# A new order by hand: the q transpose of batch 2's first group goes to the head of its DMA queue

## The chip, the cores and the metric

One core of a Trainium2 chip runs the whole program. The time is the device time of one execution in microseconds (us). Runs are compared by their median; the profile comes from one profiled execution, whose own time stands in the table below. Its "span" runs from the first to the last instruction of the program.

The core has five engines that each work through their own list of instructions in order: PE (TensorE, matrix products and transposes), ACT (ScalarE), DVE (VectorE), POOL (GpSimd, here almost only the queue that issues the loads) and SP (SyncE, here only a queue that issues DMA transposes, copies and stores). An instruction at the head of a list that waits for something holds up everything behind it on that engine.

## What is computed

Attention without softmax, followed by a two-layer network with GELU, on the attention's output:

```python
scores = scale * np.matmul(q, k.transpose(0, 1, 3, 2))
attn = np.maximum(scores, 0.0) ** 2 / S
attn_out = np.matmul(attn, v)                      # 8 batches, 12 heads, 448 positions, 64 wide
x = attn_out.transpose(0, 2, 1, 3).reshape(B * S, H * D)   # 3584 x 768
h = x @ w_in                                       # 768 -> 2048
g = 0.5 * h * (1.0 + erf(h * inv_sqrt2))
out = g @ w_out                                    # 2048 -> 768
```

Inputs and output are float32; the kernel computes in bfloat16 and accumulates in float32.

## The kernel before

The 12 heads of a batch are worked in three groups of four heads (g = 0, 1, 2). For one group:

- POOL loads q and k of the group (`nq`, `nk`, 224 KB each after the cast, lines 464 and 553) and v.
- q and k are transposed, so that the 64 elements of a head lie on the partitions (`qT`, `kT`). Batches 0 and 1 do it on PE (`tp`, lines 612 and 640). From batch 2 on it is done by DMA (`add_T_dma`): SP issues one DMA transpose for the group's k and one for its q (line 667). A DMA transpose of q brings only half of the heads to the partitions where they are needed, so two further copies swap the halves (`swapped`, on DVE by line 518, or on SP by lines 688 and 689).
- PE makes the scores in seven steps of four matmuls (`ps`, line 744); ACT (line 756) or DVE (line 758) takes the positive part, DVE squares it (line 765), and when all seven are squared, PE multiplies with v in 28 matmuls (`pav`, line 805). The result goes to `xT`.

The network follows a batch later: `psh` (line 857) and GELU for the first layer, `pso` (lines 1189 and 1284) for the second. These two, and for the last four batches `pb` (line 1009), use forms with fewer products and more sums, which puts additional work on DVE (`s_sb` line 1170, `t_sb` line 1120, `osb` line 1223, `part` line 1046). PE weaves the network's work of earlier batches between the attention steps of the present one.

**The order of the work.** Every piece of work is an `Op` with a number, in the order in which the code adds it: 1469 of them. The string `ORDER` lists all of them in one sequence; a word is an engine's letter (P, A, D, G for POOL, S for SP, Z for a filler on PE) and the op's number. `place` goes through the words and emits each op on the engine that the letter names. The place of a word among those of its own letter is the place in that engine's list; places of words of different letters do not matter to the chip, where only semaphores hold one engine back for another. What an op waits for (data, a free buffer) is worked out from what it reads and writes.

The ops that are named below:

| words | work | line |
|---|---|---|
| S228, S231, S234 | DMA transposes of k, batch 2, groups 0, 1, 2 ("k0", "k1", "k2") | 667 |
| S229, S232, S235 | DMA transposes of q, batch 2, groups 0, 1, 2 ("q0", "q1", "q2") | 667 |
| S399 | DMA transpose of q, batch 3, group 0 | 667 |
| D230, D233, D236 | swap copies of q, batch 2, groups 0, 1, 2 (two copies each) | 518 |
| P279, P276 | first score steps of batch 2, group 0: need k0 and D230 | 744 |
| P303 | first score step of batch 2, group 1: needs k1 and D233 | 744 |
| P327 | first score step of batch 2, group 2: needs k2 and D236 | 744 |
| P201, P225 | products with v of batch 1, groups 1 and 2, just ahead of P279 on PE | 805 |
| P216, P219 | score steps of batch 1, group 2; P245, P247 are first-layer pieces beside them | 744, 857 |
| G148, G147 | loads of q and k for batch 2, group 0 | 464, 553 |
| G270, G271 | loads of q (group 0) and k (group 1) of batch 3; they overwrite what q0 and k1 read, so they wait until those have landed | 464, 553 |
| G239, G238, G241 | loads of `wout` (two of 384 KB, one of 1536 KB, two of 384 KB) | 487 |
| D783, D583 | the last square that the product P784 (batch 5, group 0) needs; an `s_sb` sum of the network | 765, 1170 |

Before, SP's list begins S228 S235 S232 S231 S234 S229 S399: k0, q2, q1, k1, k2 and then q0. POOL has G270 right behind its last load for batch 2, and G239, G238 behind G270. DVE has D230, then D233, right behind the last squares of batch 1.

The lines that put the words to work and that issue the transposes:

```python
for word in ORDER.split():
    ...
        op, eng = self.open[int(word[1:])], names[word[0]]
...
for g in range(G):
    op = turn(k_dst(g), k_src(g), list(ld_k[b, g]))
    ...
    even = turn(q_dst(g), q_src(g), lands)
    both = sch.add(SWAP, swapped(g), [even] + after.pop(0))
```

Of the kernel before, what the change touches and what calls it, by code (L numbers as in the profile page):

```python
# [91 lines left out]
D86 P168 G119 A142 P165 D113 P90 A169 D107 P143 G126 D80 A166 D98 P114 A91 D95 P87 A144 D115 D92  # L92
G128 P171 A88 P137 A116 D89 A172 P99 D136 D138 P156 P159 A100 A157 P145 D160 A101 D167 P162 A146
G148 P186 P174 D163 G147 P251 A175 G151 D158 A187 P243 D176 G154 A252 D170 D173 P183 A244 P195
P189 G150 D184 A196 P259 D161 P253 D164 A260 A190 G123 P139 A254 G127 P198 D140 P180 P177 G153
D181 A199 D188 P216 D178 D197 P245 P219 A220 D179 A217 D185 P247 S228 A246 P210 P204 P207 A211
A208 A248 S235 D205 P261 S232 P222 P213 D200 D221 D191 A262 P192 A214 P263 S231 P255 A264 D182
D223 D206 A193 D218 P257 A256 D194 P249 D215 A258 D212 D209 P201 S234 S229 D224 D230 G270 P225
A202 G239 D233 A203 A250 P279 P276 A226 P265 G238 A280 G149 A227 P267 G152 A277 G269 A266 P291
P288 A268 P294 D289 P356 A295 D292 G271 G241 P303 A357 P285 P348 G272 D286 P350 D304 A349 G274  # L100
D296 P318 A351 P312 P300 A319 G273 P354 S399 G155 D281 P362 A355 D278 D305 P364 A363 A313 D293
P370 D287 D290 A365 D301 P358 A371 A359 P306 P282 P315 D307 P352 D236 P360 A353 P376 A361 P368
A377 A316 P366 A369 P372 A367 A283 P374 A373 D390 D284 P378 D308 D314 D391 D302 P327 A379 S398
P297 A328 P333 D392 P339 A334 P382 D298 A375 D329 A340 D317 A299 P330 P324 P309 A325 P380 D417
D320 A331 D310 A383 D311 D418 D335 P342 D341 P336 P321 D332 S402 D393 P384 A322 D400 S401 A381
A337 D326 D396 G407 D394 P387 G237 A385 A343 G409 G240 D420 S386 G275 A323 D344 S405 G408 D419
P443 D338 D388 P446 S404 A444 P421 D395 A447 G412 S389 P449 D397 P345 G411 A450 G242 D445 D403
A422 P452 P437 A346 S542 P423 D347 A453 A438 P455 D424 P440 P425 D456 A441 D442 P473 P470 A426
P461 D454 P427 D462 A474 A471 P429 D439 D457 D428 P464 P479 D430 P476 A480 D448 P431 D451 A465
D406 P433 A477 D432 D434 D472 S435 P467 P458 G415 A468 S545 G414 D469 P485 P491 A486 P509 D459  # L110
S541 D560 P513 D562 A492 S544 D561 A510 A460 P503 D563 A514 P494 S543 P500 P519 D463 A501 D481
D475 P515 A520 S548 D478 A495 A504 D493 D466 P517 S547 A516 P482 D496 A518 S436 D502 D487 P488
P497 A483 G553 P511 D498 G555 G551 P523 D489 A512 G552 D499 P525 G416 A524 D490 A484 D546 P600
A526 G410 G554 P609 P606 G413 D610 P521 G558 A607 A601 D505 G550 G557 P603 P506 A522 D604 P612
P639 D605 D507 S704 P531 A640 A613 P527 S705 D508 D602 A532 P624 A528 P618 P615 S708 D619 P529
A616 D549 P537 A530 A625 P535 A538 D626 D614 P636 A536 P627 P657 D608 A637 P533 A628 P539 D638
D620 A534 D611 A658 P564 A540 D629 P566 D659 D617 D641 A565 S707 S711 P630 P633 P621 D631 A634
S710 D632 P651 P642 D635 D567 S709 P568 D643 G715 D706 A622 P570 A623 D644 A652 G714 G717 A569
P648 G559 P666 P663 A649 P572 G718 D664 A667 G721 D571 P660 G722 P654 P645 D661 A655 G719 G716
G556 D662 G720 P769 P763 A764 A646 D650 P574 A647 D573 D665 P576 A770 D575 D580 S578 D581 P772  # L120
P778 P775 P584 A776 S836 D577 D653 D765 A779 P586 S835 A773 D668 D777 D656 A585 P766 P787 D582
P669 A767 A788 P781 P588 A670 D587 D712 A671 A782 P790 D774 D780 P796 A791 P590 D789 D768 D771
A797 P799 A589 D783 D583 P784 S842 A800 D591 P793 D801 P802 S839 A785 P592 A794 D803 S838 P594
D593 D786 D723 P596 D595 D792 P805 D837 P811 P823 S841 P674 A824 D597 D798 P672 A675 A806 D812
P678 S843 D804 D795 D807 P814 P817 S598 P808 A815 D818 A673 D724 A679 P874 P820 A809 P676 G851
D821 G849 P682 D825 D813 D822 A677 G846 A875 G844 P684 G847 A683 G850 D840 G845 A810 P826 A685
D819 P829 G713 P880 G852 D830 P680 A681 A881 D831 D827 P688 D828 P686 A689 D816 P889 P877 P832
D890 A878 P886 P904 D833 A887 A687 S947 P690 D834 G853 G848 D905 P892 P883 A893 P692 D884 A691
P901 A693 P898 P910 D888 D894 S950 P698 A911 D891 D906 P696 A699 D885 P694 A697 S946 D882 A902
D899 P702 A695 S599 S952 D725 P700 A703 D876 D726 P727 A701 D912 D903 D900 D879 P916 A728 P907  # L130
P895 D917 A908 D909 P913 P928 A896 P731 A914 D929 D918 S948 S949 A897 P729 D915 S951 S953 S579
P925 P922 P919 D926 A923 D730 P934 P931 D930 A920 P733 A921 A732 D935 A932 P735 D927 D734 D936
P940 D736 P937 P955 A938 D933 P737 D924 A941 D743 P739 A956 D738 D939 S741 P747 D744 D942 S954
D740 P958 A748 P970 P943 D959 S742 A971 D746 P964 P961 A944 D965 P749 A962 D966 A945 P973 P982
P967 D745 P751 A968 D957 D750 D960 D972 P753 A752 A974 D969 P755 D1035 A983 D754 D963 P994 P985
D975 P976 A995 D986 P979 D756 P997 A980 D984 P757 D854 A998 D1037 P759 A977 D987 A978 D758 D855
P1015 S761 P988 P1003 D760 A989 P858 D1027 S762 A1016 D981 P860 A859 D1036 D856 A1004 P991 D996
D861 P1018 P1012 D999 A1019 P862 A992 D990 P864 D1038 A1013 D993 D1005 D1017 P1021 P1000 D857
D1028 A1022 A863 P1009 D1014 P1006 A1001 P866 A1002 D1127 A1010 P1039 A1007 D865 D1023 P1056
D1020 P1041 A1040 D1030 D1008 P1058 A1057 D1011 P868 D1059 P1024 D1042 P1045 A1025 A1026 P1060  # L140
D1129 D1031 D1032 D867 P1062 P1043 P1047 D1063 A1044 D1029 P870 A1061 D1046 P1064 D1034 P1050
P1067 D1048 D1065 P1073 D1051 P1090 D1068 P1053 D1033 P1075 A1074 A1091 A1049 P1092 D1054 P1094
D1093 P1077 D1076 A1078 A1066 P1070 D871 P1079 D1071 P1096 D869 A1072 A1095 A1055 P1081 D1097
A1052 S872 S873 P1098 D1080 A1069 P1131 D1082 P1084 D1128 A1083 P1101 D1099 P1148 A1100 P1104
D1085 D1102 A1149 P1087 A1103 D1331 A1132 P1133 D1105 D1088 A1086 P1150 P1135 D1134 A1106 P1139
D1332 A1089 P1137 D1107 P1111 D1130 D1108 P1152 D1151 P1113 A1136 D1112 A1153 D1138 D1239 D1109
P1115 D1114 D1140 D1110 P1154 P1142 P1117 D1155 D1241 P1145 D1118 P1167 P1159 D1116 D1160 D1143
P1119 D1146 D1240 P1184 P1165 D1120 P1121 P1156 A1166 D1168 D1157 P1182 P1171 A1183 P1162 P1169
D1172 P1123 D1185 D1163 D1122 P1188 A1164 D1124 P1173 S1125 D1189 P1190 S1126 P1186 D1191 P1193
D1174 P1176 A1187 A1170 P1179 A1161 D1177 A1178 A1144 P1245 D1333 P1196 P1262 D1194 A1195 P1243  # L150
D1199 P1203 D1200 D1201 P1260 A1204 P1205 A1158 D1197 A1141 P1207 A1192 A1261 A1175 D1206 D1180
A1244 P1209 D1208 D1334 A1198 A1147 A1181 P1211 D1210 D1202 P1251 D1212 P1213 D1219 D1214 D1220
P1215 D1242 P1247 D1216 D1221 D1246 S1218 D1263 P1223 P1225 S1217 A1224 P1266 P1249 D1226 P1227
D1250 D1222 D1228 P1229 P1264 P1254 D1230 D1267 P1231 D1252 A1265 D1255 A1248 A1253 P1233 P1268
P1271 P1277 D1272 P1294 D1269 A1273 P1279 D1234 A1295 P1257 D1232 A1278 P1296 A1256 P1298 P1281
D1280 D1297 P1235 D1258 A1282 A1259 P1283 A1299 P1300 P1285 D1301 P1302 D1284 P1274 D1286 P1305
D1275 P1288 D1303 P1335 D1289 P1308 D1306 A1290 P1291 D1236 A1336 P1337 A1307 D1292 S1238 P1354
A1287 A1304 D1311 A1293 A1276 P1339 P1352 D1312 P1315 A1353 D1338 D1314 D1313 P1317 A1316 A1270
P1319 D1309 D1355 D1318 P1358 P1321 A1310 D1320 D1322 P1341 P1323 P1325 D1324 D1359 D1342 D1403
D1405 P1343 P1360 D1361 P1327 D1344 P1363 D1328 P1346 S1330 P1349 D1347 P1356 D1364 S1237 P1366  # L160
D1326 A1357 P1369 A1370 A1365 D1367 S1329 P1407 A1340 D1350 A1345 P1386 P1371 A1348 P1377 P1388
A1387 A1351 A1408 D1372 P1394 P1373 D1389 D1404 P1390 P1375 P1392 P1409 D1393 P1397 D1410 P1411
D1376 D1395 D1398 P1413 A1412 D1406 A1399 A1374 P1380 D1414 A1391 A1396 P1415 D1381 D1378 A1382
P1417 D1416 A1379 D1423 P1419 D1418 D1424 P1383 D1420 P1400 S1422 P1427 S1421 P1429 D1428 D1384
D1425 P1431 D1430 A1385 A1368 P1433 D1432 A1362 D1401 D1426 P1435 A1402 D1434 D1445 P1437 D1436
D1443 P1439 D1438 D1444 S1441 P1447 D1440 S1442 P1449 D1448 P1451 D1450 D1446 P1453 D1452 S1463
P1455 D1454 P1457 D1456 P1459 D1458 P1460 D1461 D1462 S1465 S1464 S1466
"""


class Op:


# [1374 lines left out]
```

## Time and profile before

| what | value |
|---|---|
| median of three runs | 370.57 us (370.29 to 372.97) |
| the profiled execution's own time | 370.31 us |
| its span | 368.6 us |
| busy share of the span | PE 97%, DVE 81%, PEld 62%, ACT 56%, POOL 17% |
| instructions | 8647 |
| HBM read, written | 45.61 MB, 11.01 MB |

How to read the views: "timeline" lines give start, duration, engine, line, what is written from what, and a count; in square brackets the idle time of the engine ahead of it and who ended it. "Windows" lines give, for a stretch, each engine's busy time with its number of instructions, PE's granted clock, the busy share of the DMA engines and GB/s. "Waits" lines give who waited for whom: us in total, times, longest. "Chain" lines are the work that ended last, in order of time: start, duration, what. SPq is SP's queue; its durations are those of issuing, not of the transfer. "DMA issues" give the us from issue to landing.

### The profile page before, as it was taken

What the parts mean: (1) busy time and instruction counts of PE and PEld (TensorE: products, weight loads), DVE (VectorE), ACT (ScalarE), POOL (GpSimd) and SP (SyncE); (2) the same over time, 40 slices, a digit from 0 to 9 for tenths busy, and PEclk for the clock granted to TensorE, in tenths of its full rate; (3) what the DMA queues carried; (4) which work ended last, traced back from release to release, by engine and by line L of the source; (5) the groups of instructions that cost most, each with busy time, mean ns of one, the idle gap of its engine ahead of it and who ended that gap; (6) DMA issues with size and microseconds to landing.
All of it is one profiled execution on the core that took longest, in us unless ns stands there. A gap on an engine that the chain in (4) does not pass through costs nothing.

```text
span 368.6 us, 8647 instructions
## 1 busy us (share of the span) xinstructions
PE 357.1 (97%) x3632; PEld 227.7 (62%) x3632; DVE 298.3 (81%) x511; ACT 205.0 (56%) x333; POOL 64.1 (17%) x101
## 2 busy tenths in 40 slices
PE   8889989999999999999999999999999999999994
PEld 7565544455554445555445555799797689687662
DVE  3998767569999978999998999999777757667672
ACT  5987766565768686866666678446036034243200
POOL 8565207150115115005100000000000000000000
PEclk9999999999999999999999999999999999999998
DMA  9999999999999999999995303002020201040232
GB/s 169 200 200 204 199 166 119 186 203 193 196 160 187 154 203 168 223 160 160 152 186 124 113 2 87 1 5 83 1 87 2 85 2 34 11 130 0 87 86 85
DMA packets 73126, 44.35 MB, mean 120 GB/s; under 512 B 38144, under 2 KB 69632, under 8 KB 73088
## 3 DMA queue, kind: packets, MB, share of 16 engines
q0 software_dynamic: 32912, 22.47, 43.3%
q1 hardware_dynamic: 39536, 20.83, 29.5%
q8 instruction: 28, 0.46, 0.5%
q10 hardware_dynamic: 640, 0.51, 0.4%
q14 instruction: 10, 0.08, 0.1%
HBM read 45.61 MB, written 11.01 MB: 154 GB/s over the span
## 4 chain that ended last, share of the span: by engine, by line
PE 90%; DMA 3%; SPq 2%; POOL 1%; DVE 1%; issue 1%; ACT 1%; DVEq 0%; POOLq 0%
PE pso L1189 33%; PE psh L857 19%; PE pb L1009 17%; PE ps L744 9%; PE pav L805 8%; PE pso L1284 3%; DMA v_sb<-in_v_dram 2%; SPq L667 2%; DMA qT<-nq 1%; POOL nk L553 1%; POOL nq L464 1%; ACT a_sq L756 0%; PE tp L640 0%; DVE a_sq L758 0%; PE tp L612 0%
## 5 line engine op out<-in xcount | busy, mean ns | idle before, releaser
L756 ACT ACTIVATE a_sq<-ps 128x896 bf16<-128x896 f32 (+1 forms) x125 | 109.8, 918 | 33.5 <-PE ps L744 33.3
L765 DVE TENSOR_TENSOR a_sq<-a_sq 128x896 bf16<-128x896 bf16 x169 | 96.8, 614 | 3.5 <-ACT a_sq L756 3.0
L857 PE MATMUL psh<-xT,win_sb 128*128 128x448 bf16 (+1 forms) x420 | 77.6, 337 | 0.6 <-issue 0.5
L857 PEld LDWEIGHTS <-win_sb 128*128 128x128 bf16 x420 | 38.8, 98 | 37.6 <-issue 9.3
L1046 DVE TENSOR_TENSOR part<-pb,part 128x448 f32<-128x448 f32 x80 | 46.8, 619 | 15.9 <-PE pb L1009 14.6
L1189 PEld LDWEIGHTS <-s_sb 128*128 128x128 bf16 x424 | 40.6, 98 | 26.8 <-issue 2.9
L758 DVE TENSOR_SCALAR a_sq<-ps 128x896 bf16<-128x896 f32 (+1 forms) x44 | 47.0, 1077 | 11.9 <-PE ps L744 11.4
L744 PE MATMUL ps<-qT,kT 64*64 64x448 bf16 (+1 forms) x756 | 48.7, 336 | 2.7 <-DVE qT L518 1.3
L867 ACT ACTIVATE h_sb<-psh 128x448 bf16<-128x448 f32 x64 | 34.7, 550 | 18.5 <-PE psh L857 18.4
L1189 PEld LDWEIGHTS <-h_sb 128*128 128x128 bf16 x312 | 29.4, 98 | 21.8 <-issue 4.6
L1009 PEld LDWEIGHTS <-win_sb 128*128 128x128 bf16 x384 | 36.8, 98 | 2.3 <-issue 0.4
L1189 PE MATMUL pso<-wout_sb,h_sb 128*128 128x384 bf16 x208 | 38.1, 326 | 0.0
L1189 PE MATMUL pso<-t_sb,s_sb 128*128 128x384 bf16 x208 | 38.1, 326 | 0.0
L1189 PE MATMUL pso<-wout_sb,s_sb 128*128 128x384 bf16 (+2 forms) x216 | 38.1, 320 | 0.0
L805 PE MATMUL pav<-a_sq,v_sb 64*64 64x448 bf16 (+1 forms) x756 | 36.3, 329 | 1.3 <-issue 0.9
L1055 ACT ACTIVATE h_sb<-part 128x448 bf16<-128x448 f32 x48 | 25.7, 575 | 17.6 <-DVE part L1046 17.4
L744 PEld LDWEIGHTS <-kT 64*64 64x64 bf16 x756 | 18.5, 105 | 24.3 <-issue 18.4
L1223 DVE TENSOR_TENSOR osb<-pso,p_sb 128x384 f32<-128x384 f32 x39 | 21.5, 553 | 9.8 <-PE pso L1189 7.1
L805 PEld LDWEIGHTS <-v_sb 64*64 64x64 bf16 x756 | 21.0, 107 | 12.7 <-issue 2.3
L1009 PEld LDWEIGHTS <-ws 128*128 128x128 bf16 x288 | 27.7, 98 | 1.0
L464 POOL DMA_DIRECT2D nq<-in_q_dram x24 | 17.8, 740 | 51.5 <-DMA qT<-nq 38.4
L520 ACT CAST xT<-pav 128x448 bf16<-128x448 f32 (+1 forms) x40 | 18.8, 501 | 12.0 <-PE pav L805 11.5
(58 smaller groups left out, 316.7 us busy)
## 6 DMA issues: line engine op xcount, KB each, us to landing
nk<-in_k_dram POOLq DMA_DIRECT2D x23, 224.0 KB, 8.7
nq<-in_q_dram POOLq DMA_DIRECT2D x21, 224.0 KB, 9.2
v_sb<-in_v_dram POOLq DMA_DIRECT2D x5, 672.0 KB, 13.3
out_dram<-osb SPq DMA_DIRECT2D x8, 336.0 KB, 3.2
v_sb<-in_v_dram POOLq DMA_DIRECT2D x9, 224.0 KB, 9.4
out_dram<-osb SPq DMA_DIRECT2D x7, 288.0 KB, 3.3
out_dram<-osb SPq DMA_DIRECT2D x8, 240.0 KB, 2.8
win_sb<-in_moe_w_in_dram POOLq DMA_DIRECT2D x8, 192.0 KB, 9.0
```

The lines of the kernel that those rows point to most:

```text
L744: nc.tensor.matmul(ps[64 * j : 64 * j + 64, e, x * w : x * w + w], kT[r, g, i * 128 + 64 * j : i * 128 + 64 * j + 64], moving, start=True, ...
L756: A.activation(ar, ps, AF.Relu, scale=c_att)
L758: V.tensor_scalar(ar, ps, c_att, 0.0, op0=mybir.AluOpType.mult, op1=mybir.AluOpType.max,)
L765: V.tensor_mul(box["a2"][:, :, :used], ar, ar)
L805: nc.tensor.matmul(pav[0][o2 : o2 + 64, e, :w], vt[b][r, 2 * g + e, bass.ts(i, D)], box["a2"][r, y, o : o + w], start=(i == 0), stop=(i == ...
L857: nc.tensor.matmul(ph[:, x * n : x * n + n], win_sb[:, kd, bass.ts(m + x, 128)], xT[b][:, kd, c], start=(kd == 0), stop=(kd == KD - 1),)
L867: A.activation(h_ring()[:, m : m + nm, o + c.start : o + c.stop], box[0][:, :S].rearrange("p (x n) -> p x n", x=nm), AF.Gelu,)
L1009: nc.tensor.matmul(bank[name][:, y, z * HS : z * HS + HS], w[:, k, bass.ts(mm, 128)], right()[:, k], start=first and k == 0 and z == 0, st ...
L1046: V.tensor_add(get(to), ps(name), get(other))
L1055: A.activation(h_ring()[:, m : m + 2, o + half[c].start : o + half[c].stop], src().rearrange("p (x n) -> p x n", x=2), AF.Gelu,)
L1189: nc.tensor.matmul(box[bank][:, n0:n1], left()[:, kf], right()[:, kf, n0:n1], start=bool(need) and kf == 0, stop=kf == K2 - 1, skip_group_ ...
L1223: V.tensor_add(out()[:, n0:n1], box[bank][:, n0:n1], other()[:, n0:n1])
```

## The change

Only the string `ORDER` is changed, from its ninth line on. No op is added or removed: the same 1469 numbers stand in both, and what each computes is the same.

- SP: q0 (S229) moves from the sixth place to the first; k0, q2, q1, k1, k2 keep their order behind it, and S399 follows k2. Later, a few more words of SP change places: S405 goes ahead of the store S386, S547 ahead of S548 (k and q transposes of batch 4, group 2), three transposes and two swap copies of batch 7 change places among themselves, S742 and S1329 move one place forward.
- POOL: behind G270 the big `wout` load G238 goes ahead of G239, G271 ahead of G152 and G269, and the gate G240 ahead of G407 and three others. Five more words change places later.
- PE: P219 moves ahead of P216 and P245, so that it stands beside another score step and no longer between two first-layer pieces. Some 35 further words move by one to four places between there and the end; none of them is in the stretch from P247 to P336.
- Eleven ops change their engine: the positive parts 313, 316, 319 and 613 and the copies or sums 732, 1224, 1316 go from ACT to DVE; 830, 1112, 1320 and 1448 go from DVE to ACT.
- DVE: the squares of batch 1 ahead of D230 are in another order, with D212 as the last of them instead of D224; D236 moves forward; the sum D583 goes ahead of D771 and D783. ACT and DVE have more changes of a place or two up to the end.

The core of the diff (the other lines change in the same way):

```diff
-P189 G150 D184 A196 P259 D161 P253 D164 A260 A190 G123 P139 A254 G127 P198 D140 P180 P177 G153
-D181 A199 D188 P216 D178 D197 P245 P219 A220 D179 A217 D185 P247 S228 A246 P210 P204 P207 A211
-A208 A248 S235 D205 P261 S232 P222 P213 D200 D221 D191 A262 P192 A214 P263 S231 P255 A264 D182
-D223 D206 A193 D218 P257 A256 D194 P249 D215 A258 D212 D209 P201 S234 S229 D224 D230 G270 P225
-A202 G239 D233 A203 A250 P279 P276 A226 P265 G238 A280 G149 A227 P267 G152 A277 G269 A266 P291
...
+P189 G150 D184 A196 P259 D161 P253 D164 A260 A190 G123 P139 A254 G127 P198 D140 P180 P177 D181
+A199 S229 P219 G153 D188 P216 A220 D178 P245 D197 A217 D191 P247 A246 D179 S228 P210 A248 P204
+P207 A211 S235 D205 P261 A208 D182 S232 P222 P213 D200 A262 P192 A214 D221 P263 S231 D185 D206
+P255 A264 D209 A193 D218 P257 A256 D194 P249 D223 A258 D224 S234 P201 D215 D212 G270 P225 D230
+A202 G238 A203 A250 G239 P279 P276 A226 D233 P265 A227 A280 G149 P267 G271 A277 G152 A266 P291
...
-P669 A767 A788 P781 P588 A670 D587 D712 A671 A782 P790 D774 D780 P796 A791 P590 D789 D768 D771
-A797 P799 A589 D783 D583 P784 S842 A800 D591 P793 D801 P802 S839 A785 P592 A794 D803 S838 P594
...
+P669 A767 D587 A788 D712 P781 P588 A670 D780 A671 D768 A782 D789 P790 P796 A791 P590 D774 D583
+A797 D771 P799 A589 D783 P784 S842 A800 D591 P802 D801 P793 S839 A785 P592 A794 D803 S838 P594
```

## The prediction

> **What bounds the kernel now.** I read the page first, for the engine that carries the time:
>
> ```profile
> PE 357.1 (97%) x3632; PEld 227.7 (62%) x3632; DVE 298.3 (81%) x511; ACT 205.0 (56%) x333; POOL 64.1 (17%) x101
> PE 90%; DMA 3%; SPq 2%; POOL 1%; DVE 1%; issue 1%; ACT 1%; DVEq 0%; POOLq 0%
> ```
>
> PE is busy for 97% of the span and is 90% of the chain that ended last. So a gain has to come out of an idle time of PE (or a costlier sequence on it), and a loss is whatever makes PE idle. The windows say where PE is idle (columns: stretch, length, then busy time of PE, PEld, DVE, ACT, POOL, PE's clock, DMA share, GB/s):
>
> ```profile
> 45.00:52.00 7.00, 6.99 (x58) 3.24 (x60) 6.99 (x13) 5.03 (x9) 0.00 (x0) 1.00 1.29 193
> 52.00:56.00 4.00, 2.70 (x52) 1.39 (x44) 1.13 (x4) 1.86 (x4) 0.58 (x1) 1.00 0.55 96
> 56.00:80.00 24.00, 24.00 (x166) 11.25 (x164) 14.52 (x22) 14.68 (x25) 11.31 (x17) 1.00 1.20 170
> 150.00:200.00 50.00, 50.00 (x504) 25.24 (x501) 47.57 (x77) 33.51 (x52) 6.52 (x11) 1.00 1.11 169
> 200.00:250.00 50.00, 50.00 (x509) 33.84 (x506) 48.97 (x84) 31.59 (x51) 0.00 (x0) 1.00 0.17 49
> ```
>
> PE idles in 52 to 56 and then not at all: the other stretches are full, and so are those not shown up to 363. The clock is 1.00 throughout. So all that this change can win lies at 52 to 56, and it has 300 us of full PE in which to lose it. From 150 to 250 DVE is 97% busy too. The waits and the chain of that place (30 to 60, and 50 to 60 us):
>
> ```profile
> POOL nq L464 <- DMA qT<-nq: 15.5, 1, 15.5
> ...
> DVE qT L518 <- DMA qT<-nq: 2.8, 1, 2.8
> ...
> PE ps L744 <- DVE qT L518: 1.3, 1, 1.3
> ```
>
> ```profile
> 50.30 1.30 SPq L667
> 51.59 0.05 issue
> 51.64 0.02 SPq L667
> 51.66 0.03 issue
> 51.69 3.16 DMA qT<-nq
> 54.85 0.02 issue
> 54.87 0.39 DVE qT L518
> 55.26 0.03 issue
> 55.29 0.40 DVE qT L518
> 55.69 0.04 issue
> 55.73 0.57 PE ps L744 x6
> ```
>
> q0 is the last of six transposes on SP: issued at 51.69, landed at 54.85, swapped by DVE until 55.68, and only then can PE go on with batch 2. POOL's next load waits for the same landing.
>
> **The change, part by part.** The sum is made against the profiled execution, 370.31 us (span 368.6, 1.7 around it), which is 0.3 under the median of 370.57.
>
> *q0 first on SP.* Its source was loaded by the DMA issued at 31.69, which took 8.2 us by the DMA issues: there at 39.9. SP's first transpose stands at 41.17 and SP is free before it, so q0 is issued at 39.9 and k0 at 41.2, still when its own load (32.42 + 8.7) is there. From issue to landing, window by window, the six took 8.8, 7.3, 6.1, 3.4, 3.6 and 3.2 us: k0 49.97, q2 50.7, q1 51.5, k1 52.3, k2 53.9, q0 54.9. They land in the order of issue, and the first not before the last load of POOL (39.21 + 9.6 = 48.8). So I keep the places and change the names: q0 49.9, k0 50.7, q2 51.5, q1 52.3, k1 53.9, k2 54.9. Every one of the five is a place later (0.8 to 1.6 us; the issue itself takes 1.3). q2's swap is not due before 71.44, and k2's first reader stands at 79.76 on PE: nothing. k0 must be there for P279, q1 for D233, k1 for P303; these are checked below. S399, next on SP, waited for its own load and keeps its place.
>
> *The stall.* DVE has done its last square at 52.06 (the group of seven that starts at 48.14 and takes 3.92) and then waits 2.81. With q0 there at 49.9 the two copies run 52.06 to 52.87. D233 follows, with q1 there at 52.3. PE is done with P225 at 54.05 (51.21 + 2.84) and finds q0 swapped and k0 landed: the idle 1.26 goes. The eight matmuls behind it took 0.98, from 55.31; eight such take 0.57 elsewhere, for instance at 60.53:
>
> ```profile
> 51.21 2.84 PE L805 MATMUL pav<-a_sq,v_sb 64*64 64x448 bf16 x56
> 55.31 0.98 PE L744 MATMUL ps<-qT,kT 64*64 64x448 bf16 x8 [1.26 <-DVE qT L518]
> ...
> 60.53 0.57 PE L744 MATMUL ps<-qT,kT 64*64 64x448 bf16 x8
> ```
>
> P276 waited inside for the second copy (until 55.68), and 0.41 more goes. Together 1.67. If D230 were late all the same, the stall would be what is left of it: nothing as long as q0 lands before 53.0.
>
> *P219.* At 40.25, 40.54, 41.80 and 42.11 PE goes from a score step to a first-layer piece, back, and again. In the chain of the whole span three score steps in a row (`ps` x12) take 0.69 and two take 0.50, so 0.19 each and 0.12 for the row; two first-layer pieces (`psh` x12) take 2.38 and one 1.24, so 1.14 each and 0.10 for the row. With P219 beside P216 there is one row less of either kind: 0.22, taken as 0.20, and PE gets to P279 at 53.85. The squares that P225 needs are the same in another order, the last again at 52.06 or before; PE comes to P225 at 52.36 (51.21 + 1.35 - 0.20): covered. ACT, which waited 2.35 for P219 (until 42.23), gets it earlier. The other moves on PE change no such pair: nothing.
>
> *POOL.* Its load behind q0 waited 15.50, until 55.42; now q0 lands at 49.9 and the loads of batch 3 and `wout` begin 4.9 earlier. None was late for PE before (no idle PE after 55.3), so this wins nothing, but it puts loads beside the last transposes. k1 is the one with a near reader: P303 at 60.53, now 1.87 earlier, at 58.66. Bounds for k1's landing: 53.9, its place with nothing beside it, and 50.3 + 12.4 = 62.7, from the transpose of q issued at 86.10 beside loads; the next one, at 59.54 behind three `wout` loads, took 11.5. I take 55: four of six are through by 52.3, and in the slices of the DMA view (35 to 62) the engines were full again only at 57.9, 2.5 us after POOL's load of 55.42; the new one, at 50.5, bites at 53. Cost 0, cover 3.7 us. DMA: Bandwidth & Descriptors in the Trainium skill says under Queues, rings and completion order that each DMA engine takes turns between queues, a packet at a time. By that rule alone k1's last stretch (53 to 53.9) would take twice as long and it would land at about 54.8, an estimate that leaves the sum as it is; the 8.8 us of the first transpose behind loads speak against so even a sharing.
>
> The other reorderings on POOL and SP concern transfers that have 3 to 20 us to their readers, with all loads ahead by up to 4.9: nothing. The nearest is batch 4's q of group 2, now behind its k on SP: landed at 132.07 before (117.56 + 14.5) as the second of the pair, its swap then has its turn at about 130. With the POOL loads spread earlier I take 130; cost 0 to 2, taken as 0.
>
> *ACT to DVE.* Three positive parts (1.08 each by the row at 66.97) go to DVE between 62 and 76. DVE has 9.5 idle of 24 there, 3.28 of it a wait for `wout`, which now lands earlier: nothing. Single ones later are 0.5 to 1.1 in stretches with a few us idle.
>
> *D583 ahead of D783.* Here DVE sets PE's pace:
>
> ```profile
> 156.83 3.30 DVE L765 TENSOR_TENSOR a_sq<-a_sq 128x896 bf16<-128x896 bf16 x6
> 160.05 0.68 DVE L1170 TENSOR_TENSOR s_sb<-h_sb,s_sb 128x1024 bf16<-128x1024 bf16 x1
> ```
>
> The last of six squares ends at 160.13, and PE starts P784, which needs it, at 160.04: no slack. Now the sum stands ahead of it: 0.60 (160.05 to 160.65, where the next starts) lost on PE. Bounds: 0 if DVE comes there earlier against PE than before, 0.68. I take 0.60, since DVE's timeline shows only 0.2 idle from 140 to there.
>
> Sum: 370.31 - 1.67 - 0.20 + 0.60 = 369.04, so **369.0**, 1.3 under the profiled execution and 0.4% under the median.
>
> **The rivals.**
>
> *Given back (370.3).* DVE is 97% busy from 150 to 250 and gets more work (3.2 us at 62 to 76, 1.1 near 129); if it comes out of 139 to 250 no earlier than before, PE waits there for all of the 1.87 it had won. For it: P784 and two more products with v start within 0.1 of their last square. Against it: DVE itself waited for PE at 138.84 (0.8) and 197.4 (0.9), so its clock starts anew from PE.
>
> *k1 late: slower.* If k1 lands behind the `wout` loads, PE stands at P303, in order, and nothing makes it up. It decides from a landing at 58.66 + 1.27 = 59.9. With 61.8 (50.3 + 11.5) the stall is 3.1 and the time 372.2; with 62.7 it is 373.1; with the longest, 14.5, 375.2. For it: every transpose issued beside POOL's loads took 8.8 to 14.5. Against it: those were issued behind megabytes of loads, k1 stands ahead of most.
>
> *The move does nothing.* q0 in front is issued 12 us earlier but could stay behind POOL's loads and land at 53 or later: then part of 1.67 remains, 369.5 to 370.5. k0's own 49.97 speaks against it.
>
> *All kept.* DVE comes to P784 early: 368.4.
>
> **How the numbers follow.** The forecast 0.45 (368.7 to 369.5), given back 0.20, k1 late 0.12, nothing 0.05, all kept 0.08, and 0.10 for a stall that I don't see among some sixty changed places (370.5 to 376). The range 368.3 to 372.6 leaves out about half of k1 late, a third of the unseen and the lower end of all kept. About 1% is what a measurement of this kernel can tell from no change: faster is under 366.9, which only a part of all kept and errors reach, 0.02; slower is over 374.3, 0.05 of k1 late and 0.06 of the unseen, 0.11; within it 0.87.
>
> **What would show it.** SP begins with qT at 39.9; qT lands near 50; DVE's copies start at 52 with no wait on the DMA; PE has no idle of 1.26 near 54, and its eight `ps` matmuls take 0.57; POOL's nq load goes at 50.5, not 55.4; k1 lands before 58.7; PE shows 0.6 idle before a `pav` near 158. An idle of PE before `ps` at 58 to 63 would be k1 and make me wrong, as would idle PE spread over 100 to 250 (DVE).

## The result, and the profile after

The changed kernel takes 368.62 us (median of 12 runs, 368.07 to 374.1); the kernel before, beside it, 370.43 (12 runs, 369.75 to 372.97). The ratio is 0.9937, 95% interval 0.9912 to 0.9962: 0.6% faster. One execution, the one of 374.1, ran in a slow state at a mean granted clock of 0.987 and is left out of the ratio. The interval leaves out 1, so the gain is told apart from no change, although it is within the 1% that the prediction set as the bound of what can be told. The forecast was 369.0. The profiled execution of the changed kernel took 369.34 (span 367.5).

The page of the changed kernel, the lines of busy time and of the chain:

```profile
PE 357.1 (97%) x3632; PEld 228.9 (62%) x3632; DVE 301.6 (82%) x514; ACT 202.6 (55%) x330; POOL 64.0 (17%) x101
PE 93%; DMA 2%; POOL 1%; issue 1%; ACT 1%; DVE 0%; DVEq 0%; POOLq 0%
```

PE's busy time is the same to a tenth, and its share of the chain grew from 90% to 93%: SP's queue, which was 2%, is gone from it. The same windows as before, and the waits from 30 to 60 us:

```profile
45.00:52.00 7.00, 7.00 (x54) 3.19 (x46) 6.62 (x11) 5.57 (x9) 0.30 (x1) 1.00 1.38 138
52.00:56.00 4.00, 4.00 (x70) 2.34 (x70) 3.89 (x7) 2.43 (x6) 3.79 (x5) 1.00 1.06 146
56.00:80.00 24.00, 24.00 (x177) 11.45 (x179) 17.35 (x23) 12.78 (x22) 9.97 (x14) 1.00 1.30 196
150.00:200.00 50.00, 50.00 (x504) 25.34 (x503) 46.76 (x77) 34.17 (x54) 5.87 (x11) 1.00 1.06 159
200.00:250.00 50.00, 50.00 (x512) 34.20 (x510) 48.96 (x85) 30.95 (x49) 0.00 (x0) 1.00 0.19 55
```

```profile
POOL nq L464 <- DMA qT<-nq: 10.7, 1, 10.7
...
POOL nk L553 <- DMA kT<-nk: 2.6, 1, 2.6
```

From 52 to 56 PE is now busy for 4.00 of 4.00 (2.70 before), and POOL for 3.79 (0.58): POOL's loads, which waited 15.5 for q0, now run beside DVE's swap copies. DVE's own wait for q0 (2.8) is gone from the list. A new wait is there: G271 for k1's landing. Behind 34 us PE shows no idle of 0.1 anywhere. PE's rows there:

```profile
41.84 0.55 PE L744 MATMUL ps<-qT,kT 64*64 64x448 bf16 x8
...
52.00 2.84 PE L805 MATMUL pav<-a_sq,v_sb 64*64 64x448 bf16 x56
54.67 0.55 PE L744 MATMUL ps<-qT,kT 64*64 64x448 bf16 x8
```

P279 and P276 take 0.55, where they took 0.98 behind an idle of 1.26.

The prediction expected 0.60 to be lost at P784. PE's row there before, then DVE's row of the last two squares (D783 is the second) and PE's row now:

```profile
160.04 1.49 PE L805 MATMUL pav<-a_sq,v_sb 64*64 64x448 bf16 x28
```

```profile
158.52 1.15 DVE L765 TENSOR_TENSOR a_sq<-a_sq 128x896 bf16<-128x896 bf16 x2
159.06 1.49 PE L805 MATMUL pav<-a_sq,v_sb 64*64 64x448 bf16 x28
```

D783 now ends at 159.67, 0.61 behind the start of the product (0.09 before), and the product takes 1.49 as before: nothing is lost.

**How much that is, and why two profiles cannot simply be subtracted.** Up to the pair P216, P219 both kernels have the same work on PE, but this execution reached the pair at 41.84, the one before at 40.25. That is not the change: in the fourteen profiled executions of this study the pair starts between 39.38 and 41.84, and the changed kernel itself started it at 39.98 when it ran again. What varies are the first 34 us: PE's idle there adds up to between 3.7 and 5.5, part of it for the first loads, and the first record of a granted clock of 1.00 stands between 3.95 and 7.02 (at 4.64 in the execution before, at 6.99 in this one). So I count from the start of the pair to the start of PE's last product (P1460). Before: 362.63 - 40.25 = 322.38. After: 361.64 - 41.84 = 319.80. The change took out 2.58, in these places:

| stretch on PE | before | after | gained |
|---|---|---|---|
| start of the pair to P247 | 1.86 | 1.64 | 0.22 |
| P247 to P201 | 9.10 | 8.52 | 0.58 |
| P201 to the work behind P276 (P265) | 5.02 | 3.16 | 1.86 |
| P265 to P303 | 4.30 | 4.30 | 0 |
| P303 to P1460 | 302.10 | 302.18 | -0.08 |

Most of the 0.58 ahead of P201 sits in two rows of twelve score matmuls, before and now:

```profile
43.37 1.02 PE L744 MATMUL ps<-qT,kT 64*64 64x448 bf16 x12
45.67 0.97 PE L744 MATMUL ps<-qT,kT 64*64 64x448 bf16 x12
```

```profile
44.72 0.76 PE L744 MATMUL ps<-qT,kT 64*64 64x448 bf16 x12
46.66 0.77 PE L744 MATMUL ps<-qT,kT 64*64 64x448 bf16 x12
```

The start of the pair, later by 1.59 in this execution, hides that much of it: the two profiled executions are 0.97 apart. The medians, 1.81 apart, lie between 0.97 and 2.58.

### The profile page after: what moved, and what is told of

Its sections match the earlier page's. It is cut to its first block, busy times and chain, and to the rows that moved or that the text cites. A ratio compares the mean times of both kernels' runs of the same rounds, so it can differ in the third digit from the quotient of the medians.

```text
span 367.5 us, 8638 instructions
## 1 busy us (share of the span) xinstructions
PE 357.1 (97%) x3632; PEld 228.9 (62%) x3632; DVE 301.6 (82%) x514; ACT 202.6 (55%) x330; POOL 64.0 (17%) x101
## 4 chain that ended last, share of the span: by engine, by line
PE 93%; DMA 2%; POOL 1%; issue 1%; ACT 1%; DVE 0%; DVEq 0%; POOLq 0%
PE pso L1189 33%; PE psh L857 20%; PE pb L1009 18%; PE ps L744 10%; PE pav L805 9%; PE pso L1284 3%; DMA v_sb<-in_v_dram 2%; POOL nk L553 1%; POOL nq L464 1%; ACT a_sq L756 0%; PE tp L640 0%; PE tp L612 0%; DVE xT L518 0%; ACT h_sb L867 0%; DVE osb L1223 0%
## 5 line engine op out<-in xcount | busy, mean ns | idle before, releaser
L756 ACT ACTIVATE a_sq<-ps 128x896 bf16<-128x896 f32 (+1 forms) x122 | 107.2, 917 | 33.6 <-PE ps L744 33.5
L758 DVE TENSOR_SCALAR a_sq<-ps 128x896 bf16<-128x896 f32 (+1 forms) x47 | 50.3, 1077 | 9.1 <-PE ps L744 8.6
L1055 ACT ACTIVATE h_sb<-pb 128x448 bf16<-128x448 f32 x16 | 8.4, 542 | 32.2 <-PE pb L1009 32.2
L553 POOL DMA_DIRECT2D nk<-in_k_dram x23 | 16.5, 717 | 50.8 <-DMA kT<-nk 47.2
## 6 DMA issues: line engine op xcount, KB each, us to landing
v_sb<-in_v_dram POOLq DMA_DIRECT2D x5, 672.0 KB, 11.8
```

Of the source, the lines that this page charges most:

```text
L756: A.activation(ar, ps, AF.Relu, scale=c_att)
L758: V.tensor_scalar(ar, ps, c_att, 0.0, op0=mybir.AluOpType.mult, op1=mybir.AluOpType.max,)
L1055: A.activation(h_ring()[:, m : m + 2, o + half[c].start : o + half[c].stop], src().rearrange("p (x n) -> p x n", x=2), AF.Gelu,)
```

## The experiments

My theory after this reading: the late landing of q0 is all that mattered; P219 gives its 0.2 and some waits hidden inside PE's rows; the D583 term of the prediction was wrong, because a product with v does not need its last square at its start; and with the stall gone the next thing to be late is k1. The rival: the other moved words carry part of the gain. (The prediction and the expectations call them sixty. Compared engine by engine, at least 203 words change their place and 11 their engine, S229 and P219 among them, so the others are some 210.) The runs in one table (start of the pair, landings of q0 and k1, idle of PE behind 34 us, and start of the pair to P1460, all in the profiled execution):

| kernel | pair | q0 | k1 | idle of PE, place | pair to P1460 | median (runs) |
|---|---|---|---|---|---|---|
| before | 40.25 | 54.85 | 52.33 | 1.26, q0 | 322.38 | 370.43 (12) |
| the change | 41.84 | 51.13 | 57.90 | none | 319.80 | 368.62 (12) |
| e1 q0 alone | 40.79 | 50.31 | 58.14 | 1.32 at 132.9 | 322.15 | 368.34 (12) |
| e2 P219 alone | 39.67 | 55.89 | 53.28 | 3.59, q0 | 326.67 | 372.07 (12) |
| e3 both | 39.98 | 49.97 | 58.95 | 1.10, k1 | 321.11 | 368.56 (11) |
| e4 q0 back to last | 39.93 | 54.78 | 52.30 | 2.31, q0 | 322.72 | 371.13 (12) |
| e5 D783 late | 39.98 | 50.25 | 56.84 | 1.18 at 158.7 | 321.58 | 370.19 (10) |
| e6 k1 last | 39.92 | 49.96 | 64.62 | 0.33, q0's swap; 6.35, k1 | 328.73 | 376.59 (6) |
| e7 loads behind k1 | 39.71 | 49.86 | 55.18 | none | 319.81 | 368.82 (10) |
| e8 three words | 39.96 | 50.05 | 58.75 | 1.06, k1 | 320.93 | 369.04 (12) |
| e9 pair of batch 4 back | 39.38 | 50.54 | 57.26 | 0.23, k1 | 320.17 | 368.46 (7) |
| e10 k1 fourth, loads behind | 40.78 | 50.82 | 53.68 | none | 319.91 | 367.79 (6) |
| e11 and v first | 40.23 | 50.07 | 52.70 | none | 319.80 | 367.61 (6) |
| e12 the change again | 39.98 | 50.03 | 56.60 | 0.33, q0's swap | 320.73 | 368.39 (12) |

The kernel before ran beside them with medians of 370.76 (e1 to e4), 370.95 (e5 to e8, on another chip than the rest of the experiments) and 371.87 (e9 to e12).

### e1: q0 alone

```diff
-P247 S228 A246
+P247 S229 S228 A246
...
-S234 S229 D224
+S234 D224
```

> The kernel before with one word moved: S229 (q0) ahead of S228 on SP; nothing else differs. Theory (the gain at 54 us is the late landing of q0 and nothing else): q0 lands near 50 to 51, PE shows no idle ahead of P279, the eight score matmuls there take 0.57 instead of 0.98, and the time falls by 1.7 to 1.9, to about 368.6. P216 to P247 stay as before (1.86 from the start of P216 to the start of P247). Rival (the other sixty moved words bring the gain, or are needed to keep it): the stall goes, but PE idles later, and the time stays within 0.5 of before (370.4). k1 should land by 56 to 58, ahead of P303 at about 58.7.

Measured: 368.34, ratio 0.9923 (0.9895 to 0.9951). The stall at 54 is gone, and the rest of the change is not needed for it; PE is busy from 52 to 56 without a gap:

```profile
52.00:56.00 4.00, 4.00 (x70) 2.15 (x63) 3.77 (x6) 2.68 (x6) 4.00 (x6) 1.00 1.10 140
```

The eight score matmuls of P279 and P276 take 0.66 and not the 0.57 expected: q0's second copy took 1.13 beside POOL's issues (see e7). k1 landed at 58.14, a little later than expected, and still ahead of P303 (59.33).

The median moved by at least as much as with the whole change (2.42 and 1.81), so the other words are worth nothing that the times can tell. The profiled execution, with 370.63 the longest of its twelve (the others took 368.13 to 369.26), shows what can follow:

```profile
134.20 0.38 PE L744 MATMUL ps<-qT,kT 64*64 64x448 bf16 x4 [1.32 <-DMA kT<-nk]
```

PE came to P657 at 132.9 and found k of batch 4, group 2 (S547) not landed: it came at 134.16, 17.7 us after its issue. Before, it landed at 132.07 and PE was there at 133.91, so 1.84 of slack; a gain of 1.8 upstream uses up just that.

### e2: P219 alone

```diff
-D188 P216 D178 D197 P245 P219 A220
+D188 P219 P216 D178 D197 P245 A220
```

> The kernel before with P219 moved ahead of P216 on PE, q0 still last on SP. Theory: PE saves 0.2 between P216 and P247 and, if it is this move that also frees the 0.58 seen between P247 and P201, comes to P279 up to 0.8 earlier, only to wait longer for q0, which lands when the DMAs let it: idle of PE ahead of P279 grows from 1.26 to 1.5 to 2.1, and the time is that of before (370.4) within 0.3. Rival (PE's own work is what counts): 369.6 to 370.2. If only 0.2 is saved up to P201, the 0.58 comes from other moved words.

Measured: 372.07; ratio to before 1.0006 (0.9972 to 1.0039). On PE the move does what it should: from the pair to P247 1.64 instead of 1.86, and from P247 to P201 8.61 instead of 9.10. So this one word brings 0.49 of the 0.58 that I had not priced. It brings no time, as the theory said, since q0 lands at 55.89, long after PE has come (52.76). But the loss was not expected: PE idled 3.59 for the 1.5 to 2.1 expected. PE's rows and its windows around the wait:

```profile
56.35 1.38 PE L744 MATMUL ps<-qT,kT 64*64 64x448 bf16 x8 [3.59 <-DVE qT L518]
57.66 4.66 PE L857 MATMUL psh<-xT,win_sb 128*128 128x448 bf16 x12
```

```profile
50.00:56.00 6.00, 2.76 (x56) 1.47 (x57) 1.25 (x4) 1.86 (x4) 0.00 (x0) 0.96 0.94 183
56.00:60.00 4.00, 3.65 (x15) 1.44 (x16) 1.70 (x4) 2.16 (x3) 3.54 (x5) 0.50 0.52 67
60.00:64.00 4.00, 4.00 (x25) 1.45 (x23) 1.06 (x2) 1.96 (x3) 3.57 (x5) 0.70 1.08 140
64.00:68.00 4.00, 4.00 (x35) 1.61 (x34) 4.00 (x6) 1.91 (x5) 1.42 (x2) 1.00 1.28 187
```

Behind an idle of 3.59 the granted clock is 0.50 (the column before the DMA share), and it is back at 1.00 only in the window from 64 on. Twelve `psh` matmuls take 4.66 (2.44 at full clock). From P265 to P303 PE took 6.58 instead of 4.30: 2.28 lost to the clock, more than the stall of the kernel before. The eight score matmuls that end the idle lost some 0.4 to it as well (P279 to P265 1.31 instead of 0.92).

### e3: both words

```diff
-D188 P216 D178 D197 P245 P219 A220 D179 A217 D185 P247 S228 A246
+D188 P219 P216 D178 D197 P245 A220 D179 A217 D185 P247 S229 S228 A246
...
-S234 S229 D224
+S234 D224
```

> The kernel before with both words moved, S229 ahead of S228 and P219 ahead of P216, and none of the other sixty. Theory: the two gains add up, since no wait stands between them any more: 1.7 to 1.9 for the stall and 0.2 to 0.8 for P219, so 367.8 to 368.5, no slower than the changed kernel (368.6). Rival: the later moved words of the change are worth something by themselves, and this kernel is slower than the changed one by 0.5 or more.

Measured: 368.56, 0.1 above the range expected; ratio 0.9925 (0.9897 to 0.9952), lowest 367.42. Two of the moved words give what all of them give as far as the times tell; the rival's loss of 0.5 or more is not seen. That P219 adds to q0 alone (368.34) is not seen in the times either. In PE's rows it brings 0.72 up to P201, and this execution gave it back at k1. PE came to P303 at 57.89, and there the next wait stands:

```profile
58.99 0.57 PE L744 MATMUL ps<-qT,kT 64*64 64x448 bf16 x8 [1.10 <-DMA kT<-nk]
```

k1 had landed at 58.95. This is the prediction's slower rival, in a small dose.

### e4: q0 back to last, the rest of the change kept

```diff
-A199 S229 P219
+A199 P219
...
-D224 S234 P201
+D224 S234 S229 P201
```

> The changed kernel with S229 put back behind S234, all the other sixty words as in the change. Theory: q0 lands last of the six again, near 55, and PE, which now comes to P279 0.8 earlier than in the kernel before, waits 1.9 to 2.3 there; the time is 370.3 to 371.0, so all of the gain hangs on this one word. POOL's loads behind q0 wait until about 55 again and k1 lands near 53 to 54. Rival (the later order has a gain of its own): 369.0 to 369.8.

Measured: 371.13, 0.1 above the range expected; ratio to before 1.0015 (0.9982 to 1.0049): all of the gain is gone. PE idled 2.31 ahead of P279, q0 landed at 54.78, and the clock stayed at 1.00.

```profile
55.25 0.98 PE L744 MATMUL ps<-qT,kT 64*64 64x448 bf16 x8 [2.31 <-DVE qT L518]
```

With e1 this settles it: the gain hangs on the one word S229.

### e5: D783 late

```diff
-D783 P784 S842 A800 D591 P802 D801 P793
+S842 A800 D591 D801 D783 P784 P802 P793
```

> The changed kernel with the square D783 put behind the sum D591 and the square D801 on DVE, so that it ends about 161.6 (D801 starts at 160.32 by ACT, ends 160.95, and D783 takes 0.62), 2.5 after PE is ready to start P784 (159.06). Theory (a product with v reads its seven squares in order, so the last is due only 6/7 of 1.32, 1.13 us, after its start, at 160.19): PE loses 1.3 to 1.5 inside the product, all of it at the end: 370.0. Rival (my prediction's reckoning, no slack: all squares are due at the start): PE loses 2.5, and 371.1. In the rows of the profile: P784 starts at its place and its 28 matmuls take 2.9, or PE idles 2.5 ahead of them.

Measured: 370.19, ratio 0.9962 (0.9931 to 0.9994). PE's rows at P784:

```profile
157.42 1.29 PE L805 MATMUL pav<-a_sq,v_sb 64*64 64x448 bf16 x21
159.90 0.57 PE L805 MATMUL pav<-a_sq,v_sb 64*64 64x448 bf16 x7 [1.18 <-DVE a_sq L765]
```

The product starts at 157.42, although its last square ends at 159.85, and works 21 of its 28 matmuls before it stops. The code says why: the loop goes over seven positions i and, inside, over two halves e; from batch 2 on position i of half e reads square (7e + i) // 2, so the last square, 6, is first read at i = 5, e = 1. The matmul that waited would have started at 158.37, 0.95 after the product's start. It started 1.53 late, and from P784 to P1460 PE lost 1.56 against the change (204.14 to 202.58). My estimate of 1.13 for the due time was too late by 0.2, hence 1.3 to 1.5; the prediction's reckoning would have given 2.5.

### e6: k1 last

```diff
-P263 S231 D185
+P263 D185
...
-D224 S234 P201
+D224 S234 S231 P201
```

> The changed kernel with S231 (k1) put behind S234 (k2), sixth on SP. Theory (place and the loads beside it set the landing): k1 takes the place in which k2 landed at 64.9, so it lands at 63.5 to 65.5; PE is ready for P303 at 59.46 and idles 4 to 6 us there; nothing makes it up: 372.6 to 374.6, more if the clock is lower after the idle. POOL's load G271 waits for k1, too. Rival (k1 would be served first as the smaller need, or PE has slack later): under 370. k2 in the fifth place lands at about 58.

Measured: 376.59 (375.98 to 377.1), ratio 1.0134 (1.0089 to 1.0180).

```profile
64.66 0.96 PE L744 MATMUL ps<-qT,kT 64*64 64x448 bf16 x8 [6.35 <-DMA kT<-nk]
```

```profile
64.00:66.00 2.00, 1.34 (x10) 0.42 (x11) 0.32 (x1) 0.00 (x0) 0.85 (x2) 0.50 1.29 193
66.00:68.00 2.00, 2.00 (x7) 0.81 (x6) 1.77 (x2) 0.00 (x0) 2.00 (x3) 0.50 1.27 190
68.00:70.00 2.00, 2.00 (x18) 0.71 (x16) 0.00 (x0) 1.09 (x2) 0.76 (x2) 0.88 1.32 200
```

The landing was as expected (64.62), the time was not: the idle of 6.35, and behind it 1.81 more (P303 to P1460 303.99 instead of 302.18) at a clock of 0.50. Nothing was made up.

### e7: the loads behind k1

```diff
-D215 D212 G270 P225
+D215 D212 G271 G270 P225
...
-G149 P267 G271 A277
+G149 P267 A277
```

> The changed kernel with POOL's load G271, which waits for k1's landing, put ahead of G270, so that POOL issues no load beside k1; G238, G239 and G270 follow about 2 us later than in the change. Theory (it is POOL's loads that made k1 land at 57.9 and not at its place of 53.9): k1 lands at 53.4 to 54.6 and k2 between 55 and 62; PE is as in the changed kernel where k1 was in time, and loses no more in executions where it was not: 368.0 to 368.6. Rival (the fifth transpose is late by its own queue): k1 at 57 to 58.5 all the same.

Measured: 368.82, ratio 0.9933 (0.9900 to 0.9965), lowest 367.22. k1 landed at 55.18, a little behind the 53.4 to 54.6 expected, and k2 at 56.00 instead of 64.91. The DMA issues from 48 to 62 us (count, median us from issue to landing), first of the change, then of this kernel:

```profile
kT<-nk SPq DMA_TRANSPOSE x2, 8.6
```

```profile
kT<-nk SPq DMA_TRANSPOSE x2, 4.2
```

So it is POOL's loads that hold up the last two transposes. PE idles nowhere behind 34, and from the pair to P1460 takes 319.81. The median did not come out lower than that of the change, which I had expected by up to 0.6; its ten runs spread from 367.22 to 370.47, and what differs in them their times don't tell.

The profile shows a second effect of the loads. DVE's swap copies of q0 and q1 in this kernel, and in the change run again (e12) with POOL's rows beside them:

```profile
51.36 0.81 DVE L518 COPY qT<-qT 64x896 bf16<-64x896 bf16 x2
52.64 0.79 DVE L518 COPY qT<-qT 64x896 bf16<-64x896 bf16 x2 [0.47 <-DMA qT<-nq]
```

```profile
51.62 3.27 DVE L518 COPY qT<-qT 64x896 bf16<-64x896 bf16 x4
```

```profile
50.60 0.72 POOL L464 DMA_DIRECT2D nq<-in_q_dram  x1 [11.03 <-DMA qT<-nq]
51.32 2.67 POOL L487 DMA_DIRECT2D wout_sb<-in_moe_w_out_dram  x3
```

Four copies take 1.60 while POOL is still, and 3.27 while POOL issues loads. One copy is 0.39 by itself. In the eight kernels with q0 first whose loads are not held back, 28 of the 32 copies of q0 and q1 take 0.46 to 1.15. Where POOL issues less densely it is rarer: of the 67 other swap copies that stand beside an issue in the fourteen traces, 11 take more than 0.45, and a copy that lies wholly within one issue often takes its 0.39. DVE's squares (0.62) and positive parts (1.09) take the same with and without POOL's issues. In these rows, then, a semaphore is not the only thing by which one engine holds up another. In e12 q0's second copy ended at 53.45 instead of about 52.4, and PE waited for it: P279 to P265 took 1.18 instead of 0.49.

### e8: three words

```diff
-S548 D478 A495 A504 D493 D466 P517 S547 A516
+S547 S548 D478 A495 A504 D493 D466 P517 A516
```

This stands on top of the two words of e3.

> The kernel before with three words moved: S229 ahead of S228, P219 ahead of P216, and S547 (k of batch 4, group 2) ahead of S548 (its q). Theory: with q0 early, PE comes to P657 about 1.5 to 2 us earlier, and k of batch 4's group 2, second of its pair (landed 132.07 before, 134.16 in the run of q0 alone, where PE idled 1.32 for it), is the next thing to be late; first of its pair it lands near 123 and PE shows no idle at 132. The time is that of the whole change or a little better, 367.5 to 368.6, with a k1 stall of up to 1.1 at P303 as in the run of two words. Rival: the other sixty words are worth something, 369.0 or more.

Measured: 369.04, ratio 0.9925 (0.9892 to 0.9958); above the range expected, and at the rival's 369.0. The ratio to the kernel before, which took 370.95 beside this run, is that of e3 and no worse than that of the change (0.9937), so the time does not speak for the rival. PE idled 1.06 for k1 (58.75), as in e3, and not at 132. Against e3 the times tell nothing.

### e9: the pair of batch 4 back

```diff
-P517 S547 A504 D478 D466 G552 P488 A518 S548 P482
+P517 S548 S547 A504 D478 D466 G552 P488 A518 P482
```

> The changed kernel with one pair put back: S548 (q of batch 4, group 2) again ahead of S547 (its k). Theory (the change of this pair, which my prediction costed at nothing, keeps the gain from being given back): k lands second again, 11.5 to 17.7 us after its issue, at 130 to 134, and PE comes to P657, which needs it, at 132.7: an idle of 0 to 1.4 at 132, and a median 0 to 1 above the changed kernel's. Rival (the pair does not matter): k lands before 131 and the rows from P303 to P784 take the same 99.6 as in the change.

Measured: 368.46, ratio 0.9912 (0.9880 to 0.9945), profiled 367.21. The theory falls. k, second of its pair again, landed at 121.39, nine us before PE needed it (130.64), so it was not this swap that keeps k in time in the changed kernel. The DMA issues show another difference. In the kernel before, POOL issued the load of v of batch 4 at 117.05, just ahead of this transpose of k (117.56); in e1 at 115.62, ahead of 116.41. Here POOL issued it at 117.58, behind the transpose (115.60). In e2 and e3, too, the load went ahead of this transpose, which took 12.4 and 11.8 us from issue to landing; in e9 it took 5.8. But in e8 the transpose of k went 0.3 ahead of the load and still took 10.7, so the order of the two is not all of it. The load's place was not tried by itself.

### e10 and e11: a version without either wait

```diff
-P207 A211 S235 D205
+P207 A211 D205
...
-P263 S231 D185
+P263 S231 S235 D185
...
-D215 D212 G270 P225
+D215 D212 G271 G270 P225
...
-G149 P267 G271 A277
+G149 P267 A277
```

e11 has one more move, at the very start:

```diff
-A16 G121 P11 P17 G2 D12
+A16 G2 G121 P11 P17 D12
```

> The changed kernel with two moves: S235 (q2) behind S231 on SP, so that k1 is fourth, and POOL's load G271, which waits for k1, ahead of G270. Theory: k1 lands at 52.5 to 54.5, 4 us ahead of P303; q2 and k2 land by 57; PE has no idle after 34; the time is that of the changed kernel where k1 was in time and better where it was not: 367.2 to 368.6. Rival (PE's early loads, not k1, make what differs from run to run): no difference to the changed kernel, 368.3 to 369.

> The kernel of the run before, and on POOL the first load of v (G2) ahead of the load G121 of k of batch 1, so that v lands about 0.7 earlier. Before, PE waited 0.45 to 0.81 for this v near 13.5, and 0.85 to 1.33 behind that near 19. Theory: the first idle goes and what follows starts earlier, 0.4 to 1.0 off the time, 366.8 to 368.0. Rival (ACT, busy without a pause from 11.7 to 19.9, sets the pace there): the idle only moves to the second place and the time stays.

Measured: e10 367.79, ratio 0.9896 (0.9860 to 0.9933); e11 367.61, 0.9897 (0.9856 to 0.9938). In e10 k1 landed at 53.68, 4.7 before P303; the four swap copies took 0.39 each, and PE showed no idle behind 34. In e11 the wait of PE for v near 13.5 (0.21 to 1.30 in the others) fell to 0.11, but the one near 19 stayed (1.12), and the pair started at 40.23, within the others' spread: a gain from it is not shown. Both beat the kernel before by more than the change did in its own run, but the intervals overlap, so that they beat the change is likely and not shown by the times. What the rows do show is that in these three executions, with the pair at 39.71 to 40.78, the gain did not depend on when PE came out of the first loads: 319.81, 319.91 and 319.80 from the pair to P1460 in e7, e10 and e11, against 319.80 and 320.73 in the two executions of the change.

### e12: the change again

> The changed kernel itself once more, beside the two versions before it. Expected: median 368.3 to 369.0; k1 lands 56.8 to 58.5 and the margin to P303 is between 0 and 1.7, depending on where PE comes out of the early loads (first-layer piece P141 at 22.2 to 23.9); no idle of PE behind P225.

Measured: 368.39 (367.64 to 371.56), ratio 0.9919 (0.9892 to 0.9946). k1 landed at 56.60, 0.2 earlier than expected and 1.7 before P303. The other miss is the 0.33 of idle for q0's swap, told under e7. PE came early to the pair here (39.98), so the things that are late count: 0.93 of the 2.58 was lost again, 0.70 of it up to P265.

## Why the prediction was right and where it was wrong

- **The stall (1.67).** Right. Measured 1.86 in the first execution of the change (5.02 to 3.16) and 1.17 in e12 (3.85), where POOL's issuing slowed the copies. The prediction had the two copies at their undisturbed time, "52.06 to 52.87", and did not count that the loads which q0 sets free fall just beside them. The kernel before had shown it once: of its four copies from 54.87 on, the third, beside POOL's issues from 55.42 on, took 0.62.
- **P219 (0.20).** Measured 0.22. Not priced: 0.49 to 0.58 between P247 and P201, which e2 shows to come mostly from this same word. It was to be seen before: the timeline has two rows of twelve score matmuls there with 1.02 and 0.97, where 0.76 is usual. PE waited inside these rows, and a group's busy time hides such waits.
- **D583 ahead of D783 (0.60 lost).** This is the step that failed. The prediction read that the square ends at 160.13 and the product starts at 160.04 as "no slack", and called the sum in front of it "0.60 lost on PE". That a product *starts* before its last square is done was the sign that it does not need it yet. By e5 the square is due 0.95 behind the start, so the slack was 0.86, and 0.34 of it is left in the change (square at 159.67, due at 160.01). Measured loss: none. Without this term the sum is 368.4, the figure of the rival "all kept" (0.08); the medians are 368.62 and 368.39. That rival's reason was not what happened: the last square came not earlier against PE but 0.52 later (0.61 behind the product's start, where it had been 0.09), and the product did not need it yet.
- **What a measurement can tell (about 1%).** This bound was too wide. The interval of the ratio is 0.9912 to 0.9962, some 0.25% to either side, so a gain of 0.6% stands clear of no change; on this bound rested the 0.87 for a time that cannot be told from no change.
- **The sum.** It promised PE 1.27 (1.67 + 0.20 - 0.60). PE's rows gave 2.58 in the first execution and 1.65 in e12. The 1.31 missing from the first are the 0.60 that was not lost, the 0.58 that was not priced, 0.21 more for the stall and P219, less 0.08 behind P303. That the forecast of 369.0 lies only 0.4 from the median, and the sum without the D583 term only 0.2, is in part luck: what the sum leaves out (the 0.58, the slower copies, k1, and the first 34 us) happens to offset in part.
- **The order of landings.** q0, k0, q2 and q1 were right to about 2 us: q0 49.9 to 51.1 for 49.9. k1 was mis-sized: 56.6 to 59.0 in the seven executions with POOL free and k1 fifth, for a forecast of 55. k2, forecast at 54.9, landed at 63.5 to 64.9; that cost nothing, as its reader is late.
- **Work moved to DVE, and given back (370.3).** P303 to P1460 took 302.18 for 302.10. DVE, 97% busy, gave back 0.08 at most; the rival falls, and the price of nothing was right.
- **k1 late.** The rival's mechanism is real, but it is no matter of all or nothing at 59.9: PE also comes earlier than the 58.66 of the prediction, so that k1 cost 1.10, 1.06 and 0.23 in three of those seven executions and nothing in the others. For its longest landing, 64.8 (50.3 + 14.5), the prediction had a stall of 6.1. In e6, at the last place, k1 landed at 64.62 and PE idled 6.35: the stall was priced right, and the 1.81 by the clock behind it was left out.
- **The pair S547, S548 (0).** Right for the changed kernel, by e9.

The prediction measured its gain against one execution of the kernel before, 370.31, with a stall of 1.26. In others the stall can be longer, since in the three traces with q0 last it lands at 54.8 to 55.9 whether PE comes at 54.05 or at 52.76, and somewhere between 2.31 (e4) and 3.59 (e2) the clock begins to add to it. Of the 79 runs of the kernel before that stand beside the experiments 30 had a mean clock of 0.995 or less, and each of these took over 371.2, as did 7 of the other 49 (one of them with 2059.86). Of the 98 runs of kernels with q0 first (without e6) 3 had such a clock, and one of these took over 371. That the low clocks of the kernel before come from its q0 stall is concluded from e2, where the trace shows it, and was not seen in a trace of the kernel before itself.

## What to carry to other kernels

When a stall is taken out, everything behind it comes earlier, so list the margin of each transfer with a near reader and expect those below the gain to become the next wait; here k1 was. Ask what the freed queue will do in the same microseconds: POOL's loads, let go some 4 to 5 us earlier, delayed two transposes and slowed the copies, and holding them behind the one landing that matters kept the whole gain on PE in three traces (e7, e10, e11). And read an operand's due time from the consumer's loop, not from its start.

## What the runs showed of the hardware

- **The clock behind an idle PE.** Idles of 1.26, 1.32 and 2.31 left the granted clock at 1.00; those of 3.59 and 6.35 were followed by 0.50 for 4 to 6 us, at a cost of 2.28 (and some 0.4 ahead of that) and 1.81. By the trace's clock records it fell 2.82 and 3.33 us into these two idles and stayed at 0.50 for 6.83 us in both; values between, as 0.70 and 0.88, are means over a window. The Trainium skill, TensorE: Matmul & The Clock Gate, says under What's actually happening that the clock is either full or half, and falls to half behind an idle window of about 3.4 us. The two values and the lengths of the five idles agree; the falls came a little sooner after the start of the idle.
- **POOL's issuing slows DVE's copies.** 0.39 alone, 0.46 to 1.15 for 28 of 32 beside a dense row of POOL's DMA issues of 0.7 to 1.2 each; held back (e7, e10, e11), 0.39 for all twelve. SBUF — State Buffer in the Trainium skill says under SBUF: two separate sides that GpSimd and some forms of DVE instruction share one pair of ports, which is locked and not split, so that one of them waits. The rows agree in part: here it was DVE that waited, but copies that lay wholly within one issue took 0.39 as well. That this lock is the cause is not shown by a run.
- **Transposes beside loads.** Behind q1, k1 took 2.57 more with no load of POOL issued (e7) and 3.89 to 6.36 with them. DMA: Bandwidth & Descriptors in the Trainium skill says under Queues, rings and completion order that engines take turns between queues. By that rule, which the prediction weighed, the 2.57 would become some 5.1, an estimate in the middle of what was measured. The prediction's 54.8 came out too early because it doubled only the last 0.9 (53 to 53.9), from the landings of the old order. Where the 1536 KB load of `wout` was issued ahead of the 384 KB ones, k1 landed at 56.6 to 57.9, and in the other order at 58.1 to 59.0; why is open. Near the pair this is what the traces show of the other moved words: k1 cost 1.10 and 1.06 in e3 and e8, which have the old order of these loads, and 0.23 at most in the kernels with the new one and k1 fifth.
